# A second copy of 64 rows: made ahead of the first transposes, or later by one copy between partitions

## The chip, the cores and the metric

The kernel runs on one core of a Trainium2 chip. The core has a matrix engine (TensorE, PE), a vector engine (VectorE, DVE), a scalar engine (ScalarE, ACT), a general engine (GpSimd, POOL) and a synchronisation engine (SyncE, SP) that mostly issues DMA transfers. Each engine works through its own queue of instructions in order; between engines they wait on semaphores. The on-chip memory has 128 partitions. A tile of shape [128, n] has n elements in each of them, and TensorE contracts over partitions. TensorE writes into PSUM, from which VectorE or ScalarE copies the results.

The metric is device time in microseconds (us) of the whole program, lower is better.

## The reference, cut to what matters

x has 2048 rows of D = 576 columns. The layer norm of x, xn, feeds two branches:

```
xn = layernorm(x)
q  = xn @ wq                       # 32 heads of 128 columns; wq is 576 x 4096
s  = softmax(q k^T / sqrt(128)) v @ wo   # 16 key heads, last 512 keys, each used by 2 query heads
h  = shift(gelu(layernorm(xn) @ w1)) @ w2
x1 = xn + h
b  = x1 + gelu(layernorm(x1) @ w3) @ w4
out = x + s * silu(b)
```

All inputs and the output are bf16.

## The kernel before, in words

The 2048 rows are worked on in 4 blocks of 512 (QB). Within a block there is one slot for each of the 32 query heads, so the attention stage has 128 slots, numbered u; after it comes the MLP stage (w3, w4) in a loop of its own. A slot of the attention stage holds, in an order that is written out by hand for SP, POOL and PE: the four score matmuls of head u, with the projection of q for head u + 1 behind the first of them; eight matmuls and again eight that multiply the exponentials of head u - 1 with V; and fill work (transposes of keys, wo, w1, w2). `at(u, fn)` puts a function into slot u, right behind the projection. VectorE and ScalarE aren't ordered by hand there; a planner orders them, and `tc.high_priority` moves an instruction ahead.

The projection contracts over 576 columns of xn. That is four chunks of 128 and a rest of 64. xn is held transposed in `xT_b[0]` or `xT_b[1]`, five chunks [128, 512] each, used by blocks in turn. The fifth chunk has the 64 rest columns of xn in partitions 0 to 63. In partitions 64 to 127 it has the same 64 rows a second time: from slot 7 on, `rest_q` multiplies the rest of two heads at once, one on the lower and one on the upper 64 partitions (heads 8 and later; `two = u >= PLAIN`, PLAIN = 8). The first eight heads use the fifth chunk with all 128 partitions, and their wq tile has zeros in partitions 64 to 127 (`load_wq` with j < 2, and the memsets of `wq_b` at line 319). So for them the upper half of xT counts nothing, as long as it is finite.

In block 0 the second copy is made ahead of the transposes. `ln1_first` normalises the four row tiles of block 0 into `xn_b[0]`, whose rows have 640 columns: 0 to 575 are xn, and 576 to 639 are the second copy of 512 to 575. For tiles 0 and 1 it is made by GpSimd (line 389, from x, with the same mean and factor), for tiles 2 and 3 by one VectorE copy (line 393). `tr1_first` (line 406) then transposes each row tile with TensorE in five chunks of 128 columns, the fifth with both copies, into PSUM; `xT_first` copies the five chunks to `xT_b[0]` (lines 412 and 414). In between and after, `keys_first` transposes the keys of four heads (line 422).

The opening is ordered by hand on all engines: warm-up matmuls on TensorE, transposes of tiles 0 and 1, keys 0 and 1, transposes of tiles 2 and 3, keys 2 and 3, then `stage_q(0)` and `stage_q(1)` (line 458). On POOL the order is: memsets of `xnn_b`, `wq_b`, `v_sb`, `w1r_sb`, `w1_sb`, `w2_sb` (lines 317 to 330), the two small copies of line 389, two loads of V for key heads 4 and 5 (line 288; slot 0's `load_v(2)`), and then the gated loads of later slots (`late`, line 307, waits for an exponential of its slot). On SP the loads of the opening are issued in the order: two row tiles of x, the first keys, wq's first block (lines 265 and 268), V, wq's second block, V, keys.

In the later blocks the second copy comes with the layer norm (`twice=True`), and the transposes are DMA transposes.

## Time and profile before

| | us |
|---|---|
| median of 3 runs | 831.66 |
| lowest and highest of them | 831.16 to 831.76 |
| the profiled execution, device time | 831.61 |
| its span, first to last instruction | 829.8 |
| granted TensorE clock, mean | 0.998 |

The profile gives busy times of each engine, the chain of waits that ended last, and the instructions in order of time. PEld is the loading of weights into TensorE, which overlaps its matmuls. In the timeline a row is one instruction or several of a kind, merged; its duration reaches from the first one's start to the last one's end. Matmuls are pipelined, so the end of one lies behind the start of the next. A DMA row on SP or POOL (SPq, POOLq) is the issue of a transfer; the time to landing stands in the view of the DMA queues, where q1 is SP's queue, q10 ScalarE's and q0 POOL's, each with its packets, MB and the share of the 16 DMA engines' time that it took.

### The profile page before, as it was taken

How to read it: one execution, taken by the hardware profiler on the slowest of the kernel's cores; microseconds unless marked ns; L12 is line 12 of the kernel's file. 1: busy time of each engine (PE TensorE's matmuls, PEld its weight loads, DVE VectorE, ACT ScalarE, POOL GpSimd, SP SyncE). 2: the span in 40 equal slices, each digit the busy share in tenths (PEclk: the TensorE clock that was granted, in tenths of full speed). 3: DMA queues.
4: the chain of work that ended last, by engine and by line, in shares of the span. 5: the costliest groups of instructions: out<-in, count | busy, mean ns of one | idle time of the engine just before them, and what ended most of it. 6: DMA issues, size and time to landing. Idle time of an engine off the chain costs nothing.

```text
span 829.8 us, 19512 instructions
## 1 busy us (share of the span) xinstructions
PE 816.6 (98%) x7888; PEld 471.4 (57%) x7974; DVE 472.8 (57%) x1431; ACT 455.3 (55%) x819; POOL 97.2 (12%) x164
## 2 busy tenths in 40 slices
PE   9999999999999999999999999999999999999996
PEld 6666654655554566555465655555555555555555
DVE  5778645678885357964356773043246636646333
ACT  6888853588773368983467983042243333334610
POOL 5353223010100111110001100000000000000000
PEclk9999999999999999999999999999999999999999
DMA  7988992363471145762045365992010411230101
GB/s 200 191 186 178 191 174 74 83 123 72 114 136 49 42 90 124 141 135 55 7 84 133 95 112 109 312 320 34 2 29 17 98 36 45 48 87 17 43 15 47
DMA packets 141024, 83.95 MB, mean 101 GB/s; under 512 B 107504, under 2 KB 133808, under 8 KB 140928
## 3 DMA queue, kind: packets, MB, share of 16 engines
q1 hardware_dynamic: 130128, 53.01, 31.8%
q0 software_dynamic: 9408, 28.15, 12.7%
q10 hardware_dynamic: 1392, 1.48, 0.5%
q8 instruction: 64, 1.05, 0.5%
q14 instruction: 32, 0.26, 0.1%
HBM read 49.17 MB, written 9.44 MB: 71 GB/s over the span
## 4 chain that ended last, share of the span: by engine, by line
PE 96%; DMA 1%; issue 1%; DVE 1%; ACT 1%; POOL 0%; ACTq 0%; POOLq 0%; DVEq 0%
PE ph L891 14%; PE po L496 14%; PE pswo L520 13%; PE sc L479 13%; PE psq L458 13%; PE pm L928 11%; PE pm L1093 4%; PE ph L572 3%; PE pm L891 2%; PE psx L623 2%; PE pswr L520 2%; PE pr L928 1%; PE psq L443 1%; PE sc L443 1%; DMA wo_sb<-in_A_wo_dram 1%
## 5 line engine op out<-in xcount | busy, mean ns | idle before, releaser
L481 ACT ACTIVATE pT<-sc 128x512 bf16<-128x512 f32 x512 | 285.5, 598 | 105.5 <-PE sc L479 97.4
L479 PE MATMUL sc<-qT,kT 128*128 128x512 bf16 x509 | 171.8, 379 | 0.1
L496 PEld LDWEIGHTS <-pT 128*128 128x128 bf16 x2048 | 134.5, 98 | 54.8 <-issue 9.8
L496 PE MATMUL po<-v_sb,pT 128*128 128x129 bf16 x2048 | 158.3, 220 | 0.2
L458 PE MATMUL psq<-xT_b,wq_b 128*128 128x512 bf16 x469 | 126.1, 379 | 2.7
L891 PE MATMUL ph<-xT_b,w_s 64*128 64x512 bf16 x976 | 127.1, 376 | 0.4 <-DVE hx L907 0.4
L928 PE MATMUL pm<-w_s,h 64*128 64x512 bf16 x864 | 122.3, 377 | 0.0
L520 PE MATMUL pswo<-wo_sb,oT 128*128 128x512 bf16 x500 | 114.9, 379 | 0.6
L501 DVE TENSOR_TENSOR o<-po,ri_b 128x256 bf16<-128x256 f32 x256 | 107.9, 421 | 6.1
L909 ACT ACTIVATE h<-ph 128x512 bf16<-128x512 f32 x67 | 39.4, 597 | 130.5 <-PE ph L891 130.5
L928 PEld LDWEIGHTS <-h 64*128 64x128 bf16 x1728 | 70.9, 94 | 55.4 <-issue 0.4
L520 PEld LDWEIGHTS <-oT 128*128 128x128 bf16 x1024 | 65.3, 98 | 56.7
L928 PE MATMUL pr<-w_s,h 64*128 64x64 bf16 x864 | 90.3, 189 | 0.2 <-ACT h L909 0.2
L891 PEld LDWEIGHTS <-w_s 64*128 64x128 bf16 x1152 | 57.3, 94 | 48.9 <-issue 0.8
L458 PEld LDWEIGHTS <-wq_b 128*128 128x128 bf16 x520 | 50.5, 98 | 59.8 <-issue 1.5
L907 DVE COPY hx<-ph 128x512 f32<-128x512 f32 x55 | 38.0, 692 | 70.0 <-PE ph L891 70.0
L500 DVE RECIPROCAL ri_b<-po 128x2 f32<-128x2 f32 x256 | 42.2, 165 | 50.6 <-PE po L496 46.6
L479 PEld LDWEIGHTS <-kT 128*128 128x128 bf16 x512 | 47.0, 98 | 26.6 <-DVE qT L466 0.6
L265 POOL DMA_DIRECT2D wq_b<-in_A_wq_dram x30 | 23.2, 775 | 292.0 <-PE sc L479 285.3
L466 DVE TENSOR_TENSOR qT<-psq,rq 128x512 bf16<-128x512 f32 x60 | 41.4, 689 | 25.4 <-ACT pT L481 19.0
L468 DVE CAST qT<-psq 128x512 bf16<-128x512 f32 x44 | 30.3, 689 | 35.1 <-PE psq L443 28.0
L881 DVE TENSOR_SCALAR fence<-ph,ph 1x1 f32<-1x1 f32 x61 | 12.8, 210 | 49.7 <-PE ph L891 49.1
(152 smaller groups left out, 747.7 us busy)
## 6 DMA issues: line engine op xcount, KB each, us to landing
wq_b<-in_A_wq_dram POOLq DMA_DIRECT2D x30, 512.0 KB, 4.6
wo_sb<-in_A_wo_dram POOLq DMA_DIRECT2D x8, 576.0 KB, 5.1
w_s<-in_B_w_dram SPq DMA_DIRECT2D x9, 512.0 KB, 7.0
w_s<-in_B_w_dram SPq DMA_DIRECT2D x10, 288.0 KB, 5.2
x_dram<-x SPq DMA_DIRECT2D x4, 576.0 KB, 3.5
x<-x_dram SPq DMA_DIRECT2D x4, 576.0 KB, 4.3
w_s<-in_B_w_dram SPq DMA_DIRECT2D x4, 576.0 KB, 8.0
s_b<-s_dram SPq DMA_DIRECT2D x4, 576.0 KB, 5.3
```

The costliest lines, as they stand in the source:

```text
L458: nc.tensor.matmul(psq[:, :], lhsT=w[:, kc, hh * Dh:(hh + 1) * Dh], rhs=xT_b[qb % 2][:, kc, :], start=(kc == 0 and not (two and hh == 1)), ...
L466: nc.vector.tensor_tensor(out=qT[:, :], in0=psq[:, :], in1=rq_t.pop(u)[:, :], op=ALU.add)
L479: nc.tensor.matmul(sc[:, :], lhsT=kT[:, g, kc * P:(kc + 1) * P], rhs=qT_t[u][:, :], start=True, stop=True)
L481: nc.scalar.activation(out=pT[:, :], in_=sc[:, :], func=ACT.Exp, scale=SCALE)
L496: nc.tensor.matmul(po[:, j, :], lhsT=pTs[kc][:, tt * P:(tt + 1) * P], rhs=v_sb[:, g, kc, 0:Dh + 1], start=(kc == 0), stop=(kc == KCH - 1))
L500: nc.vector.reciprocal(out=ri, in_=po[:, :, Dh])
L501: nc.vector.tensor_tensor(out=o[:, t0:t0 + 2, :], in0=po[:, :, 0:Dh], in1=ri.unsqueeze(2).to_broadcast([P, 2, Dh]), op=ALU.mult)
L520: nc.tensor.matmul(ps, lhsT=oT_t[qb * Hq + h][:, tt, :], rhs=wo_sb[:, h, lo:hi], start=(h == 0), stop=(h == Hq - 1))
L891: nc.tensor.matmul(ps[i][:, :], lhsT=lhsT, rhs=xT[half, kc, :], start=first, stop=last, skip_group_check=True)
L907: nc.vector.tensor_copy(out=src[:, :], in_=ps[i][:, :])
L909: nc.scalar.activation(out=h3[:, :], in_=src[:, :], func=ACT.Gelu_apprx_tanh)
L928: nc.tensor.matmul(out, lhsT=h3_t[b, fc][half, tt * P:(tt + 1) * P], rhs=w4_s[fc // WS][half, fc % WS, lo:hi], start=key not in started, s ...
```

## The change

The copies of lines 389 and 393 go. Columns 576 to 639 of `xn_b[0]` are cleared once by a GpSimd memset instead, so that the transposes bring zeros into partitions 64 to 127 of the fifth chunk. In slot 4, behind the projection of head 5, one VectorE copy `rest_twice` writes the chunk's partitions 0 to 63 to partitions 64 to 127, with high priority. In the changed program it stands on VectorE's queue right behind the cast of head 5's q, and the last projection matmul of head 6 waits for it.

```diff
-        nc.gpsimd.memset(xnn_b[:, :, D:], 0.0)
+        for w in (xn_b[0], xnn_b):
+            nc.gpsimd.memset(w[:, :, D:], 0.0)
...
             for i in range(TB):
                 if i % 2 == 0:
                     nc.vector.reciprocal(out=y[:, i:i + 2], in_=y[:, i:i + 2])
-                if i < 2:
-                    nc.gpsimd.tensor_scalar(out=xn[:, i, D:DP], in0=x[i][:, NF * P:D], scalar1=mv[:, i, 0:1],
-                                            scalar2=y[:, i:i + 1], op0=ALU.subtract, op1=ALU.mult)
                 nc.vector.tensor_scalar(out=xn[:, i, 0:D], in0=x[i], scalar1=mv[:, i, 0:1], scalar2=y[:, i:i + 1],
                                         op0=ALU.subtract, op1=ALU.mult)
-            nc.vector.tensor_copy(out=xn[:, 2:TB, D:DP], in_=xn[:, 2:TB, NF * P:D])
...
+        def rest_twice():
+            with tc.high_priority(offset=HP):
+                nc.vector.tensor_copy(out=xT_b[0][DR:P, NF, :], in_=xT_b[0][0:DR, NF, :])
...
+        at(4, rest_twice)
```

## The prediction

> **What bounds the kernel now.** I read the page first, its busy times and the shares of the chain of waits.

> ```profile
> PE 816.6 (98%) x7888; PEld 471.4 (57%) x7974; DVE 472.8 (57%) x1431; ACT 455.3 (55%) x819; POOL 97.2 (12%) x164
> PE 96%; DMA 1%; issue 1%; DVE 1%; ACT 1%; POOL 0%; ACTq 0%; POOLq 0%; DVEq 0%
> ```

> TensorE is busy for 816.6 of 829.8 us and carries 96% of the chain. So an edit is worth time where TensorE waits, and otherwise nothing. The change touches the opening and one slot near 24 us, so I read the chain there next, and then the instructions of the opening in order of time, engine by engine. Columns of the chain: start, us, what. Columns of the timeline: start, us, engine, line, operation, tiles, count, and in brackets the idle time before it.

> ```profile
> 6.86 1.38 POOL xn_b L389 x2
> 8.28 0.23 PE ps_x L406
> ...
> 10.10 1.26 PE psq L458 x5
> ```

> POOL (a memset, then from the last one on what follows, and the first of the two L288 by itself):

> ```profile
> 0.89 0.31 POOL L317 MEMSET xnn_b<- 128x256 bf16 x1
> ```

> ```profile
> 4.41 0.58 POOL L330 MEMSET w_sb<- 128x576 bf16 x1
> 6.86 1.37 POOL L389 TENSOR_SCALAR xn_b<-hb,ln_mv,nr_y 128x64 bf16<-128x64 bf16 x2 [1.86 <-DVE nr_y L387]
> 8.11 1.75 POOL L288 DMA_DIRECT2D v_sb<-in_A_v_cache_dram  x2
> ```

> ```profile
> 8.11 0.98 POOL L288 DMA_DIRECT2D v_sb<-in_A_v_cache_dram  x1
> ```

> VectorE (the two pairs of normalisations and the copies):

> ```profile
> 6.78 0.77 DVE L391 TENSOR_SCALAR xn_b<-hb,ln_mv,nr_y 128x576 bf16<-128x576 bf16 x2
> ...
> 7.66 0.81 DVE L391 TENSOR_SCALAR xn_b<-hb,ln_mv,nr_y 128x576 bf16<-128x576 bf16 x2
> 8.51 0.57 DVE L393 COPY xn_b<-xn_b 128x128 bf16<-128x128 bf16 x1
> 9.52 1.08 DVE L414 COPY xT_b<-ps_x 128x512 bf16<-128x512 bf16 x3 [0.44 <-PE ps_x L406]
> ```

> TensorE (weight loads that waited, then matmuls):

> ```profile
> 7.69 0.28 PEld L406 LDWEIGHTS <-xn_b 128*128 128x128 bf16 x5 [0.17 <-POOL xn_b L389]
> 8.28 0.10 PEld L406 LDWEIGHTS <-xn_b 128*128 128x128 bf16 x1 [0.30 <-POOL xn_b L389]
> ```

> ```profile
> 7.27 1.24 PE L406 MATMUL ps_x<-ident,xn_b 128*128 128x128 bf16 x10
> 8.35 0.61 PE L422 MATMUL ps_k<-ident,x 128*128 128x128 bf16 x8
> ...
> 9.14 0.51 PE L406 MATMUL ps_x<-ident,xn_b 128*128 128x128 bf16 x6
> ...
> 10.00 0.38 PE L458 MATMUL psq<-xT_b,wq_b 128*128 128x512 bf16 x1
> ...
> 10.98 0.38 PE L458 MATMUL psq<-xT_b,wq_b 128*128 128x512 bf16 x1
> ```

> The weight loads of the fifth transpose of tile 0 and of tile 1 stand behind the two small POOL copies (L389; idle 0.17 and 0.30). The VectorE copy (L393) ends at 9.08, and the fifth transpose of tile 2 starts 0.06 later, first of the six from 9.14. The copies out of PSUM (L414) start only when tile 3's first transposes are done, at 9.52. The first of the three ends near 9.9, and the first projection matmul starts at 10.00; its five run to the one at 10.98. From there the chain is matmul behind matmul, so a shift of the last of these five is a shift of the end, unless later waits take it up.

> **Step 1: three copies out of the transposes' way.** The pitch of transposes is (0.61 - 0.23) / 7 = 0.055 us, from the row of eight and that of one. Tile 0 starts at 7.27 as now; its fifth transpose, whose weights load at 7.69 now, starts at 7.49. Tile 1's normalisation ends at 6.78 + 0.77 = 7.55, so with the 0.06 its transposes run from 7.61 to 7.83. The eight of the keys follow from 7.89, tile 2 (the first half of the pair at 7.66, so ready near 8.1) from 8.33. Tile 3 is ready at 8.47, and its first transpose starts at 8.60. Now it starts one pitch after 9.14, at 9.20. So the transposes, the copies out of PSUM and all that hangs on them alone come 0.60 us earlier. The first projection matmul could start at 9.40, and the last of its five at 10.38.

> **Step 2: POOL's queue.** The added memset (as large as L317, 0.31 us) delays POOL's memsets by that; they end at 4.99 + 0.31 = 5.30. Nothing on the path reads what they clear before the projection at 9.4. Behind them now stand the two copies that wait for VectorE. Without these the two loads of V for key heads 4 and 5 (L288, 128 KB each), which wait for nothing else, are issued at 5.30 and not at 8.11: 2.8 us earlier, into the loads that the first projection needs.

> ```profile
> 2.69 0.48 SPq L265 DMA_DIRECT2D wq_b<-in_A_wq_dram  x1
> ```

> ```profile
> wq_b<-in_A_wq_dram SPq DMA_DIRECT2D x1, 512.0 KB, 6.7
> ...
> q1 hardware_dynamic: 1293, 0.60, 120.3%
> ...
> q1 hardware_dynamic: 1544, 0.77, 81.0%
> q0 software_dynamic: 94, 0.26, 29.3%
> ...
> q0 software_dynamic: 53, 0.16, 35.0%
> ```

> The first is the issue of the first block of wq, the second its time to landing: 2.69 + 6.7 = 9.4. The third row is SP's queue from 7.2 to 9.4 us: it fills the 16 engines (120%), with nothing from POOL. The next two are SP's and POOL's queue from 10 to 14 us, and the last is POOL's alone from 10 to 12. V's packets start 1.9 us after their issue (8.11 to 10.0), so they will start at 7.2, while wq is still arriving. Now wq lands just ahead of its use (9.4 against 10.0); with step 1 there is no slack left (9.4 against 9.40).

> What this costs is not in the trace. Lower end: 0, if the engine that lands last is not crossed (more packets on the same engines can't bring wq sooner). Upper end: all of V's time, 0.293 x 4.0 = 1.17 us on each engine. The nearest row is that of V's first two us: 0.350 x 2.0 = 0.70 us on each engine by the time wq is due; as the engines overlap packets (120%), I take 0.70 / 1.2 = 0.58. Then wq lands at 9.98, the first projection matmul starts 0.06 later at 10.04, and the last of the five, 4 pitches of 0.217, at 10.91. Against 10.98 now that is a gain of 0.07 us: the transfer takes nearly all that step 1 frees. Ends: with no delay 9.4 lets the matmul start at 9.46, its last at 10.33, and the copies bind at 10.38, a gain of 0.60; with 1.17 the last is at 11.50, a loss of 0.52. Break-even is a delay of 0.65 us.

> [...]

> **Step 3: the copy in slot 4.** One VectorE copy of 64 x 512 within SBUF, behind the cast of head 5's q.

> ```profile
> L612 DVE COPY hs<-hb 32x512 bf16<-32x512 bf16 x16 | 4.5, 283 | 0.2
> ```

> ```profile
> 23.18 0.69 DVE L468 CAST qT<-psq 128x512 bf16<-128x512 f32 x1 [0.88 <-PE psq L458]
> ```

> ```profile
> 26.03 0.69 DVE L468 CAST qT<-psq 128x512 bf16<-128x512 f32 x1 [0.88 <-PE psq L458]
> ```

> ```profile
> 24.97 1.03 PE L458 MATMUL psq<-xT_b,wq_b 128*128 128x512 bf16 x4
> ```

> The nearest copy, SBUF to SBUF with 512 columns, takes 0.28 us; the removed one (0.57) and the cast (0.69) bound it from above. Queued behind it are two reciprocals and two scalings of the attention's output, each later by as much. After them VectorE idles 0.88 us before the next cast at 26.03, which covers even 0.69. The only new wait on TensorE is that of head 6's last projection matmul, at 24.97 + 4 x 0.22 = 25.85; the copy is done at 24.2 to 24.6. Cost 0. Without that idle time its 0.28 us would delay the next cast once.

> **Sum.** 831.61 us for the profiled execution (span 829.8), less 0.07, is 831.5. The median of the runs is 831.66 (831.16 to 831.76), 0.05 above the profiled one, so nothing is added.

> **Rivals.**
> - The transfer is not delayed: gain 0.60, 831.0 us. For it: the whole of wq is nearly through by 7.2 and only stragglers land at 9.4. Against: the engines are full until then.
> - A lock between POOL and VectorE. The two 64-column POOL copies take 1.37 us beside VectorE's normalisations of nine times their columns; the small L393 takes 0.57 and ends (9.08) with POOL's first L288 (9.09). So the two seem to shut each other out. The two L288 would now run from 5.30 to 5.30 + 1.75 = 7.05 at the latest, and could hold the first normalisation (6.78) by up to 0.27. With an undelayed transfer that leaves a gain of 0.33, 831.3 us; with a delayed one it is hidden behind it. [...]
> - The transfer is delayed by more than 0.65: a loss of up to 0.52, 832.1 us. It is slower than before, but within what can be told.
> - Slower for certain: the copy in slot 4 outlasts its cover. It would have to take over 0.88 us to cost anything and 0.88 + 1.66 = 2.5 us to cost 0.2%, nine times the nearest row; then 833.3 us. I see no row for that.
> - Faster by over 0.2%: the shift lets the later slots mesh better.

> ```profile
> 13.00:510.00 497.00, 492.78 (x4196) 288.86 (x4273) 328.51 (x1038) 344.92 (x631) 88.67 (x146) 1.00 0.55 112
> ```

> TensorE idles 4.2 us (497.00 - 492.78) from 13 to 510 us. A gain of 1.7 would take 1.1 more after the opening's 0.6, a quarter of that idle time, and nothing in the change reaches it. 829.9 us.

> **How the numbers follow.** A measurement of this kernel tells about 0.2%, 1.7 us, from no change. The forecast (transfer delayed by 0.3 to 0.65) has 0.44, the undelayed transfer 0.20, the lock with it 0.05, the later transfer 0.17; all of these are within 0.2%: 0.86. The long copy has 0.08 and the better mesh 0.06. The range goes from 831.0 to 832.1 by the bounds, and 0.2 beyond each, as the runs shown spread by 0.6: 830.8 to 832.3. The forecast's own is 831.2 to 831.7.

> **What would show it.** Right: no idle time on the weight loads of the transposes, the copies out of PSUM start near 8.9, POOL's loads of V at 5.3, the first projection matmul waits for wq and starts between 9.8 and 10.1, the copy at 24 us takes 0.3 and the next cast still has idle time before it. Wrong: that matmul near 9.4 (transfer free), or later than 10.1 (transfer worse), VectorE's normalisation held at 6.8 (lock), or TensorE idle in slots 4 and 5 (copy).

## The result, and the profile after

The changed kernel takes 830.35 us in the median of 21 runs (829.65 to 831.86), the kernel before, run beside it, 831.66 (831.16 to 832.78). The ratio is 0.9984 with a 95% interval of 0.9977 to 0.999: 1.3 us faster, inside the 0.2% that was called no change, but below the predicted range (830.8 to 832.3) by 0.45 us. The profiled execution took 830.35 us with a span of 828.6, against 831.61 and 829.8: 1.26 and 1.2 less.

The opening first, in the timeline of the changed kernel (columns as in the prediction; its lines 403, 411 and 459 are 406, 414 and 458 of before):

```profile
3.59 0.82 DVE L378 BATCH_NORM_STATS2 ln_st<-hb 128x6 f32<-128x288 bf16 x2 [2.71 <-DMA hb<-in_A_x_dram]
...
5.19 1.67 POOL L288 DMA_DIRECT2D v_sb<-in_A_v_cache_dram  x2
...
6.63 0.77 DVE L389 TENSOR_SCALAR xn_b<-hb,ln_mv,nr_y 128x576 bf16<-128x576 bf16 x2
...
7.11 0.62 PEld L403 LDWEIGHTS <-xn_b 128*128 128x128 bf16 x10
...
8.14 0.60 PEld L403 LDWEIGHTS <-xn_b 128*128 128x128 bf16 x10
...
8.78 1.09 DVE L411 COPY xT_b<-ps_x 128x512 bf16<-128x512 bf16 x3 [0.51 <-PE ps_x L403]
...
9.26 0.38 PE L459 MATMUL psq<-xT_b,wq_b 128*128 128x512 bf16 x1
```

The weight loads of the transposes (L403) have no idle time any more, the copies out of PSUM start at 8.78 and the first projection matmul at 9.26, before at 9.52 and 10.00. Of these 0.74 us some 0.15 are not the change's: x landed earlier in this execution. Before, the same statistics of the layer norm started 0.15 later:

```profile
3.74 0.82 DVE L377 BATCH_NORM_STATS2 ln_st<-hb 128x6 f32<-128x288 bf16 x2 [2.86 <-DMA hb<-in_A_x_dram]
```

From the start of the first normalisation to that of the first copy out of PSUM it was 9.52 - 6.78 = 2.74 us before and is 8.78 - 6.63 = 2.15 now, so the opening gives 0.59 us. That isn't one execution's luck: the two other profiles with the old opening, taken for the experiments below, have 2.74 too, and the seven others with the freed transposes 2.15 to 2.16, but for one with 2.26. The loads of V (L288) are issued at 5.19, but their packets come late. The queue view of the changed kernel, from 4.5 to 9.3 us and then from 9.2 to 12 (queue, packets, MB, share of the 16 engines' time):

```profile
q1 hardware_dynamic: 2278, 1.46, 106.4%
...
q0 software_dynamic: 1, 0.00, 0.2%
```

```profile
q1 hardware_dynamic: 972, 0.50, 77.3%
...
q0 software_dynamic: 94, 0.26, 36.8%
```

Up to 9.3 us one packet of POOL's queue (q0) is in the record, so wq's first block has the DMA engines without V's packets. Its issue and its time to landing:

```profile
2.67 0.47 SPq L265 DMA_DIRECT2D wq_b<-in_A_wq_dram  x1
```

```profile
wq_b<-in_A_wq_dram SPq DMA_DIRECT2D x1, 512.0 KB, 6.3
```

That is 2.67 + 6.3 = 8.97, ahead of the matmul at 9.26. Slot 4 went as forecast: the copy takes 0.29 us and the next cast still has 0.64 us of idle time before it, 0.24 less than before:

```profile
22.45 0.69 DVE L469 CAST qT<-psq 128x512 bf16<-128x512 f32 x1 [0.88 <-PE psq L459]
...
23.17 0.29 DVE L427 COPY xT_b<-xT_b 64x512 bf16<-64x512 bf16 x1
...
25.30 0.69 DVE L469 CAST qT<-psq 128x512 bf16<-128x512 f32 x1 [0.64 <-PE psq L459]
```

The other half of the gain lies over 500 us later, in the MLP stage, in which nothing was changed. There ScalarE takes one half of a result from PSUM (h) and VectorE the other (hx), both behind the same matmuls. Two places of the timeline of before, at 574 and at 708 us:

```profile
574.27 0.60 ACT L909 ACTIVATE h<-ph 128x512 bf16<-128x512 f32 x1 [2.54 <-PE ph L891]
...
574.66 0.69 DVE L907 COPY hx<-ph 128x512 f32<-128x512 f32 x1 [2.03 <-PE ph L891]
...
575.38 0.63 ACT L909 ACTIVATE h<-hx 128x512 bf16<-128x512 f32 x1 [0.52 <-DVE hx L907]
...
575.40 0.54 PEld L891 LDWEIGHTS <-w_s 64*128 64x128 bf16 x7 [0.32 <-issue]
```

```profile
708.23 0.60 ACT L909 ACTIVATE h<-ph 128x512 bf16<-128x512 f32 x1 [2.54 <-PE ph L891]
...
708.62 0.69 DVE L907 COPY hx<-ph 128x512 f32<-128x512 f32 x1 [1.75 <-PE ph L891]
...
709.35 0.63 ACT L909 ACTIVATE h<-hx 128x512 bf16<-128x512 f32 x1 [0.52 <-DVE hx L907]
...
709.37 0.54 PEld L891 LDWEIGHTS <-w_s 64*128 64x128 bf16 x7 [0.32 <-issue]
```

The same places in the changed kernel:

```profile
573.65 0.60 ACT L911 ACTIVATE h<-ph 128x512 bf16<-128x512 f32 x1 [2.54 <-PE ph L893]
...
573.69 0.69 DVE L909 COPY hx<-ph 128x512 f32<-128x512 f32 x1 [1.68 <-PE ph L893]
...
574.37 0.60 PEld L893 LDWEIGHTS <-w_s 64*128 64x128 bf16 x8
...
574.41 0.63 ACT L911 ACTIVATE h<-hx 128x512 bf16<-128x512 f32 x1 [0.16 <-DVE hx L909]
```

```profile
707.27 0.60 ACT L911 ACTIVATE h<-ph 128x512 bf16<-128x512 f32 x1 [2.54 <-PE ph L893]
...
707.30 0.69 DVE L909 COPY hx<-ph 128x512 f32<-128x512 f32 x1 [1.40 <-PE ph L893]
...
708.03 0.63 ACT L911 ACTIVATE h<-hx 128x512 bf16<-128x512 f32 x1 [0.16 <-DVE hx L909]
```

Before, VectorE's copy starts 0.39 us behind ScalarE's instruction, after, 0.04 and 0.03 behind it. The next ScalarE instruction waits for the copy and is later by as much. TensorE waits too: the weight load behind it comes after 0.32 us of idle time, and the view of waits of before (us in total, times, longest) names the copy twice, where that of the changed kernel has no such row:

```profile
PE ph L891 <- DVE hx L907: 0.4, 2, 0.2
```

So the lead of the changed kernel grows at these two places: 0.62 us by the first rows (574.27 to 573.65), 0.97 by the next (575.38 to 574.41), 0.96 at 708 and 1.32 behind it (709.35 to 708.03); the end of the span keeps 1.2.

Why the copy starts late shows when VectorE's instructions are counted in the trace, from 0, with its waits that have a row of their own. In the kernel before the two late copies are numbers 1343 and 1599; they are 256 apart, and both are 63 more than a multiple of 128. In the changed kernel the same copies are 1342 and 1598, since VectorE has one wait fewer. Before, the instruction that writes new factors of the layer norm at 43.4 us (in slot 11) also had to wait for POOL, which had read the old ones for the two small copies of line 389, and that took one more wait with a row of its own, number 105. The removed and the added VectorE copy cancel out.

### The profile page after: what moved, and what is told of

It is laid out like the page before. It is cut to its first block, busy times and chain, and to the rows that moved or that the text cites. A ratio compares the mean times of both kernels' runs of the same rounds, so it can differ in the third digit from the quotient of the medians.

```text
span 828.6 us, 19597 instructions
## 1 busy us (share of the span) xinstructions
PE 820.4 (99%) x7974; PEld 470.9 (57%) x7974; DVE 472.7 (57%) x1431; ACT 455.3 (55%) x819; POOL 96.1 (12%) x163
## 4 chain that ended last, share of the span: by engine, by line
PE 99%; ACT 0%; DVE 0%; POOL 0%; issue 0%; ACTq 0%; POOLq 0%
PE po L497 14%; PE ph L893 14%; PE psq L459 14%; PE sc L480 13%; PE pswo L521 13%; PE pm L930 11%; PE pm L1095 4%; PE ph L573 3%; PE pm L893 2%; PE psx L624 2%; PE pswr L521 2%; PE pr L930 2%; PE psq L444 1%; PE sc L444 1%; PE warm L773 1%; PE pr L1095 0%
## 5 line engine op out<-in xcount | busy, mean ns | idle before, releaser
L459 PE MATMUL psq<-xT_b,wq_b 128*128 128x512 bf16 x520 | 133.0, 379 | 0.0
L521 PE MATMUL pswo<-wo_sb,oT 128*128 128x512 bf16 x512 | 116.6, 379 | 0.0
L265 POOL DMA_DIRECT2D wq_b<-in_A_wq_dram x30 | 23.3, 775 | 292.0 <-PE sc L480 285.3
## 6 DMA issues: line engine op xcount, KB each, us to landing
wq_b<-in_A_wq_dram POOLq DMA_DIRECT2D x30, 512.0 KB, 4.7
w_s<-in_B_w_dram SPq DMA_DIRECT2D x9, 512.0 KB, 7.1
```

Of the source, the lines that this page charges most:

```text
L459: nc.tensor.matmul(psq[:, :], lhsT=w[:, kc, hh * Dh:(hh + 1) * Dh], rhs=xT_b[qb % 2][:, kc, :], start=(kc == 0 and not (two and hh == 1)), ...
L521: nc.tensor.matmul(ps, lhsT=oT_t[qb * Hq + h][:, tt, :], rhs=wo_sb[:, h, lo:hi], start=(h == 0), stop=(h == Hq - 1))
```

## The experiments

The theory of the late copies: a VectorE instruction whose number leaves 63 when divided by 128 pauses for some 0.36 us if it stands right behind a wait (it starts 0.40 us behind the end of that wait and not 0.04); the change gained because it moved the two copies off such numbers by one. Its rival: the second half of the gain comes from the changed work itself, through what runs earlier or from V's loads, and one instruction more does nothing. Three kernels add one VectorE instruction that nobody needs, a memset of one element: the changed kernel with it in the opening, the old kernel with it there, and the changed kernel with it between the two places. The fourth is the changed kernel again. All four ran beside the same kernel before (831.52 us).

```diff
         with tc.manual_schedule(engines={SP, POOL, PE, DVE, ACTE}):
             mv = ln1_first()
+            nc.vector.memset(pad[:], 0.0)
```

> The changed kernel with one more VectorE instruction, a memset of one element that nothing reads, behind the first normalisations. Theory A (opening 0.60 us, plus two stalls of about 0.32 us in the MLP stage that went because VectorE's instructions moved up by one): the memset moves them back, so the copies hx near 574 and 708 us again start 0.40 us and not 0.04 us behind the wait ahead of them, TensorE loses about 0.32 us at each, and the time is 0.65 us above the changed kernel, 831.0 us; the opening is as in the changed kernel. Theory B (the rest of the gain is scatter between executions or lies in the opening): no difference from the changed kernel, 830.35 us, hx 0.04 us behind its wait.

> The kernel before with the same one memset and nothing of the change. Theory A: the copies hx leave the place at which VectorE pauses, TensorE gains about 0.32 us at each of the two, 831.0 us, though an instruction was added and the opening is the old one (first projection matmul 2.7 us or so behind the first transpose). Theory B: 831.66 us, with the two stalls of 0.32 us still there.

The late one stands in the MLP's loop instead:

```diff
+                if d == 24:
+                    nc.vector.memset(pad[:], 0.0)
```

> The changed kernel with the one memset in the MLP stage, near 670 us, between the two places. Theory A: only the second stall comes back: hx near 574 us starts 0.04 us behind its wait, hx near 708 us 0.40 us; 830.35 + 0.32 = 830.7 us. Theory B: no stall, 830.35 us.

> The changed kernel once more, for comparison on the same chip. Theory A: 830.35 us, no stall at 574 and 708 us, opening 0.52 to 0.67 us ahead of the old one at the last matmul of the first projection. Theory B: the stalls come and go from execution to execution, and are as likely here as in the kernel before.

Measured, with the numbers of the two copies counted as above, and the time from ScalarE's start to VectorE's:

```
kernel            median us   runs   ratio to before [95%]        copies no.   late by us
before            831.52       33    1                            1343 1599    0.39 0.39
changed + memset  831.14       11    0.9991 [0.9982, 1.0000]      1343 1599    0.39 0.39
changed + late    830.75       11    0.9985 [0.9972, 0.9999]      1342 1599    0.04 0.39
changed, again    830.15       11    0.9983 [0.9974, 0.9992]      1342 1598    0.04 0.04
before + memset   830.76       11    0.9991 [0.9979, 1.0004]      1344 1600    0.04 0.03
```

The two places in the timeline of the old kernel with the memset (the copy right behind ScalarE's start):

```profile
574.25 0.60 ACT L911 ACTIVATE h<-ph 128x512 bf16<-128x512 f32 x1 [2.54 <-PE ph L893]
...
574.29 0.69 DVE L909 COPY hx<-ph 128x512 f32<-128x512 f32 x1 [1.68 <-PE ph L893]
```

```profile
707.84 0.60 ACT L911 ACTIVATE h<-ph 128x512 bf16<-128x512 f32 x1 [2.54 <-PE ph L893]
...
707.87 0.69 DVE L909 COPY hx<-ph 128x512 f32<-128x512 f32 x1 [1.40 <-PE ph L893]
```

and the second place in that of the changed kernel with the late memset:

```profile
707.27 0.60 ACT L912 ACTIVATE h<-ph 128x512 bf16<-128x512 f32 x1 [2.54 <-PE ph L894]
...
707.66 0.69 DVE L910 COPY hx<-ph 128x512 f32<-128x512 f32 x1 [1.75 <-PE ph L894]
```

The lag of the copy follows its number in every kernel, with and without the change. One useless instruction makes the old kernel's median 0.76 us lower (the interval of that ratio reaches 1.0004, so its time alone would not settle it) and the changed one's 0.8 to 1.0 higher (831.14 against 830.35 and 830.15); put between the two places, it costs some 0.4 to 0.6 and brings back one late copy. The rival falls. With the late copies in both kernels, what is left of the change is 831.52 - 831.14 = 0.38 us in the medians; with them in neither it is 830.76 - 830.15 = 0.61. The traces' 0.59 for the opening lies within these.

The next three kernels ask about the parts of the change. The first keeps the two POOL copies, but lets them write a spare tile, so that V is issued as late as before while the transposes are free:

```diff
+                if i < 2:
+                    nc.gpsimd.tensor_scalar(out=spare[:, i, :], in0=x[i][:, NF * P:D], scalar1=mv[:, i, 0:1],
+                                            scalar2=y[:, i:i + 1], op0=ALU.subtract, op1=ALU.mult)
```

> The changed kernel with the two small POOL copies kept on POOL's queue, but into a spare tile that nothing reads, so that the two loads of V are issued near 8.1 us as before and the transposes don't wait. Theory S (V's packets don't start before SP's queue has emptied, near 9.3 us, whatever their issue, so the earlier issue cost wq nothing): wq's first block lands near 9.0 to 9.4 us and the first projection matmul starts near 9.3 us as in the changed kernel; V's first packet near 9.3 to 10 us. Theory T (my prediction's: V's packets start about 2 us behind their issue and take their share from wq): the first projection matmul starts earlier than in the changed kernel by up to 0.6 us. Beside that, VectorE gets back its wait on POOL in slot 7, one instruction, so by the shift of the instruction stream the copies hx near 574 and 708 us start 0.40 us behind their wait again: 830.35 + 0.65 = 831.0 us by S, 830.4 to 831.0 by T.

It took 831.01 us (10 runs; 0.9994 [0.9984, 1.0003], before beside it 831.49). POOL issues V at 8.37, and its first packet comes at 12.51, not at the 9.3 to 10 that was expected. With the POOL copies VectorE's additional wait is back (at 43.0 us, which is slot 11 and not the slot 7 of the expectation): the MLP's copies are numbers 1343 and 1599 again and late by 0.39. Set against the changed kernel with the memset, which has the same late copies and the early issue of V, it differs by 0.13 us: when V is issued is worth nothing that can be told from these medians.

The second issues V's loads early on POOL's queue, behind the memsets of `wq_b`, to force the collision that the prediction feared; it ran twice:

```diff
         for w in wq_b:
             nc.gpsimd.memset(w[DR:, NF, :], 0.0)
+        load_v(2)
...
-            if g % 2 == 0 and g >= 4:
+            if g % 2 == 0 and g >= 6:
```

> The changed kernel with the two loads of V issued behind the memsets of wq_b, near 2.9 us and not 5.2 us. Theory S: V's first packet still near 9 us, wq lands near 9.0 to 9.4 us, time as the changed kernel, 830.35 us. Theory T: V's packets from about 5 us, 1.17 us of each DMA engine taken ahead of wq, which lands near 10.2 us; the first projection matmul starts near 10.2 us, 0.9 us later than in the changed kernel, and the time is 831.2 us.

> The same kernel as v_early (the two loads of V issued near 2.8 us), once more. If V's packets, which there started 3.7 us behind their issue, take wq's time in every execution (theory T), wq's last part lands near 10 us again, the first projection matmul waits for it, and the time is 0.6 to 0.9 us above the changed kernel. If the late landing there was one slow DMA engine of one execution, wq lands near 8.5 to 9.3 us and the time is the changed kernel's, 830.2 to 830.4 us.

Times 830.40 us (10 runs; 0.9988 [0.9979, 0.9998]) and 830.56 (11 runs; 0.9988 [0.9979, 0.9997]). The first execution's timeline, the time to landing of wq's first block (issued at 2.69), and the queues from 7 to 9 us:

```profile
2.77 1.67 POOL L288 DMA_DIRECT2D v_sb<-in_A_v_cache_dram  x2
```

```profile
10.16 1.04 PE L460 MATMUL psq<-xT_b,wq_b 128*128 128x512 bf16 x4 [0.84 <-DMA wq_b<-in_A_wq_dram]
```

```profile
wq_b<-in_A_wq_dram SPq DMA_DIRECT2D x1, 512.0 KB, 7.4
```

```profile
q1 hardware_dynamic: 804, 0.29, 74.3%
...
q0 software_dynamic: 79, 0.20, 39.7%
```

V's first packet comes at 6.47 us, 3.7 behind the issue and amid SP's packets. So the thought that POOL's packets are held until SP's queue has drained falls. In this execution wq lands at 2.69 + 7.4 = 10.1 us and the first projection matmul waits 0.84 us for it, a wait of the kind that the prediction put on the change itself.

The second execution of the same edit doesn't repeat it. V's first packet comes at 6.74, and from 7 to 9 us the shares of the two queues are nearly the same:

```profile
q1 hardware_dynamic: 760, 0.32, 73.0%
...
q0 software_dynamic: 86, 0.23, 39.5%
```

```profile
wq_b<-in_A_wq_dram SPq DMA_DIRECT2D x1, 512.0 KB, 6.1
```

```profile
9.75 1.57 PE L460 MATMUL psq<-xT_b,wq_b 128*128 128x512 bf16 x6
```

wq, issued at 2.71, lands at 8.8, and the matmul at 9.75 stands 0.48 us behind the first copy out of PSUM (9.27), as in the changed kernel (9.26 behind 8.78); it is late because the second tile of x landed late (at 5.00 us VectorE's statistics had waited 0.32 us for it), ahead of V's first packet. In the nine profiles without the early issue wq lands between 8.2 and 9.4. So of the two executions in which the packets met, wq was late in one, and whether V's packets made it late, or one slow transfer of that execution, stays open. The medians lie 0.05 to 0.41 us above those of the changed kernel (830.35 and 830.15), which their intervals don't tell from nothing, and not at the 831.2 that was expected from the collision.

The third does the copy of slot 4 six times:

```diff
+                for _ in range(6):
                     nc.vector.tensor_copy(out=xT_b[0][DR:P, NF, :], in_=xT_b[0][0:DR, NF, :])
```

> The changed kernel with the copy of slot 4 made six times, 0.29 us each, 1.45 us of VectorE added in the slot. My theory (0.88 us of idle time cover it): the idle time of 0.64 us ahead of head 6's cast is used up, the cast starts about 0.8 us late, and TensorE loses at most that once; the slots after it have 0.7 to 0.9 us of idle time each and win it back on VectorE. 830.35 to 831.2 us. The rival (a copy between partitions is dear, or TensorE waits for each): TensorE stops for over 1.5 us in slots 4 and 5, over 831.9 us. hx near 574 and 708 us stays clear of the pause (five instructions further).

It took 831.72 us (10 runs; 1.001 [0.9999, 1.0022]). The expectation missed, since it looked at the next cast and not at what reads the copied rows:

```profile
24.21 1.03 PE L460 MATMUL psq<-xT_b,wq_b 128*128 128x512 bf16 x4
...
25.96 0.61 DVE L428 COPY xT_b<-xT_b 64x512 bf16<-64x512 bf16 x2
26.62 0.38 PE L460 MATMUL psq<-xT_b,wq_b 128*128 128x512 bf16 x1 [1.38 <-DVE xT_b L428]
```

All six write the rows that head 6's last projection matmul reads, and the planner put reciprocals and scalings between them, so that this matmul waited 1.38 us for the sixth. Each copy still takes 0.29 us. So a single copy isn't dear; in the changed kernel it ends at 23.46, some 1.4 us ahead of that matmul (24.88). The six copies used up this margin, which the expectation had left out.

At last the kernel before once more:

> The kernel before, a second profile. Theory A: the same two stalls, hx 0.40 us behind its wait near 574 and 708 us, 831.5 us. The distance from the issue of V's loads to their first packet was 2.0 us in the first profile of this kernel and 3.7 to 4.4 us in the others: if that belongs to the kernel it is 2.0 again, if to the execution about 4.

831.46 us (8 runs; 1.0002 [0.9992, 1.0012]). Its late copies are numbers 1343 and 1599 again:

```profile
574.46 0.69 DVE L907 COPY hx<-ph 128x512 f32<-128x512 f32 x1 [2.03 <-PE ph L891]
```

```profile
708.40 0.69 DVE L907 COPY hx<-ph 128x512 f32<-128x512 f32 x1 [1.75 <-PE ph L891]
```

It also brings the other reading that had misled: how long V's first packet takes from POOL's issue.

```
kernel             issue   first packet   between
before              8.11      10.12         2.0
before, again       7.92      10.78         2.9
before + memset     8.05      12.1          4.1
V late              8.37      12.51         4.1
changed             5.19       9.29         4.1
changed, again      5.20       9.49         4.3
changed + memset    5.19       9.58         4.4
changed + late      5.19       9.51         4.3
six copies          5.19       9.32         4.1
V early             2.77       6.47         3.7
V early, again      2.77       6.74         4.0
```

The 2.0 us of the profile before was the lowest of eleven; eight of them are about 4 or above. What sets it stays open. The other end of the prediction's meeting was a draw as well: its landing of wq at 9.4 is the latest of the nine without the early issue.

None of these kernels was faster than the changed kernel.

## Why the prediction was wrong

**Step 1, right.** No idle time on the transposes' weight loads; copies out of PSUM forecast for 8.9, seen at 8.78, with x 0.15 earlier; a gain of 0.60 forecast, 0.59 seen.

**Step 2, the failed step.** The issue of V was right (5.30 forecast, 5.19 seen). The term "V's packets start 1.9 us after their issue" came from one execution; it measured 4.1, so they started at 9.29, when wq had landed. The forecast delay of 0.58 us was 0: the first projection matmul started at 9.26, not between 9.8 and 10.1. The rival "the transfer is not delayed", with a chance of 0.20, describes what happened here, but not for the reason given for it (that wq was nearly through by 7.2): in the changed kernel V came too late to meet wq. The price of a meeting isn't borne out either: with V issued early, wq landed at 10.1 in one execution and at 8.8 in the other. Where the packets met, from 7 to 9 us of the early issue, the shares of SP's and POOL's queue were 74.3 to 39.7% and 73.0 to 39.5%, and which delay follows from such shares these two executions don't say.

**Step 3, right.** The copy took 0.29 us (0.28 forecast), cost nothing, and the cast kept 0.64 us of idle time before it.

**The missing term.** With the undelayed transfer the prediction's own sum is 831.0, and the runs gave 830.35. The other 0.65 are the two late copies of the MLP stage: about 0.35 each in the lead of the changed kernel (0.62 to 0.97, 0.96 to 1.32). The sum has no term for that stage: "nothing in the change reaches it" was said of 13 to 510 us, and what lies behind was put at nothing, unread. Its two waits could be read in the profile before, as TensorE's two waits for hx; that an instruction fewer on VectorE would take them away could not.

**The rivals that fell.** The lock between POOL and VectorE held nothing up here: POOL's issues end at 5.19 + 1.67 = 6.86, the first two normalisations start beside them at 6.63, as long after the statistics as before, and take 0.77 us together as before. The long copy: 0.29 us. The better mesh came nearest in amount (1.26 us beside its 1.7), but the second half lies in another stage and follows the numbers of two VectorE copies.

## What to carry to other kernels

Where a change moves a tuned kernel by some 0.1%, look at where the lead over the old trace grows, over the whole span, before crediting the edited place: half of this gain lay 550 us behind the edit, and one useless instruction gave it to the old kernel too. A short pause that an instruction has behind a wait, at only one or two of many equal places, may depend on its number on its engine, as the 0.39 us of the copies with numbers 1343 and 1599 did here; adding one dead instruction to either kernel tells it apart from the change itself. A latency read from one execution (here 2.0 us for a transfer to start, and 2.0 to 4.4 in eleven profiles) is one draw, and a sum that turns on it needs the range of several.

## What the runs showed of the hardware that was not expected

Shortly after the pause at 574.66 one packet moves on a queue of the kind "instruction" (at 575.3; view of the queues of before, 573 to 576 us):

```profile
q14 instruction: 1, 0.01, 1.2%
```

The queue moves 0.26 MB in 32 packets over the whole span, 8 KB each. In the trace of before one of them starts within 0.9 us behind nine of the fourteen VectorE instructions with numbers of that kind, and behind none of the thirteen half-way between (127 above a multiple of 128); in the trace of the changed kernel behind five of the fourteen and one of the thirteen. What these packets carry, and whether they have to do with the pause, no run shows: its cause stays open, and only its dependence on the number is shown. Behind each of the two pauses in the MLP stage of before, TensorE's next weight load came after 0.32 us of idle time.
